# Attention and experts in one kernel: inputs laid out by superchunk and partition, and loads, masks and set-up moved

## The chip, the cores and the metric

The kernel runs on one core of one Trainium2 chip. The metric is the device time of one execution in microseconds (us); lower is better. A core has TensorE (PE, matrix products, with weight loads shown as PEld), VectorE (DVE), ScalarE (ACT), GpSimd (POOL) and SyncE (SP), which issues loads; 16 DMA engines move data between the main memory and SBUF. Products land in PSUM.

## What is computed

Sliding-window attention over 8 batches, 8 heads, 576 positions of 64 values, then a mixture of 8 experts over the 4,608 rows of 512 values. Cut to what matters:

```python
scores = scale * np.matmul(q, k.transpose(0, 1, 3, 2))
rel = pos[:, None] - pos[None, :]
mask = (rel >= 0) & (rel < 64)
attn = softmax(np.where(mask, scores, -1e9))
x = (attn @ v), as (batch, position, 512)

logits = x @ w_gate                       # 8 experts
local_gate = sigmoid(x @ w_local)
for s in range(S):
    fresh_e = argmax(logits[b, s])
    e = fresh_e if s == 0 or local_gate[b, s] < 0.5 else prev_e
    p = softmax(logits[b, s])
    out[b, s] = p[e] * (relu(x[b, s] @ w1[e]) @ w2[e])
```

A row's expert can be that of the row before it, so the routing runs along the sequence; all is in 32-bit floats.

## The kernel before

The rows are taken in 9 superchunks (`sc`) of 512 rows, each in 4 units (`hp`), a unit being two heads. A unit makes scores (36 small matmuls), an exponential on ScalarE, a multiplication by a 0/1 mask on VectorE, and then values (32 matmuls, with a column of ones that gives the row sum); VectorE divides and writes `x`. Scores run two units ahead (`LEAD = 2`). The values product takes v twice: `va` as loaded, and `vb`, the same rows displaced by 64, which ScalarE and GpSimd copy together from `va` of this superchunk and the one before (`shift`).

The gate logits come in one of two ways. For superchunks 0 to 3, x is transposed on TensorE (`turn`), multiplied by the gate weights (`gates`) and brought back (`logits`). From superchunk 4 (`TURNED`) on the gate product of v, loaded once more in transposed form (`vtt`), is put beside v as extra columns (`spread`), so that the values product delivers the logits as well. When the logits of the first 14 chunks of 128 rows are there, the routing of the first three batches (`Router.first`) runs in small steps beside the units that follow; the experts begin after attention.

Pools and loads (cut):

```python
    cp = ctx.enter_context(tc.tile_pool(name="at_const", bufs=1))
    kp = ctx.enter_context(tc.tile_pool(name="at_k", bufs=3))
    ps_s = ctx.enter_context(tc.tile_pool(name="at_ps_s", bufs=2, space=PSUM))
    ps_x = ctx.enter_context(tc.tile_pool(name="at_ps_x", bufs=2, space=PSUM))
    ctx.enter_context(tc.manual_schedule(engines={ET.PE, ET.Activation, ET.SP}))
    ...
    def space(name, sc):
        return kp.tile([P, 4, H, width(sc)], F32, name=name, bufs=2 if name == "vb" else 3)

    def load(sc, parts):
        t = slice(sc * SC, (sc + 1) * SC)
        src = v3[t] if sc < TURNED else v4[t.start - TURNED * SC:t.stop - TURNED * SC]
        for part in parts:
            if part == "turned":
                vtt = vts[sc] = kp.tile([P, HP, WIN + SC], F32, name="vtt", bufs=1)
                a = 0 if sc == TURNED else WIN
                at = (sc - TURNED) * SC + a
                nc.sync.dma_start(out=vtt[:, :, a:], in_=vt[:, :, at:at + WIN + SC - a])
            elif isinstance(part, tuple):
                ...
                nc.sync.dma_start(out=vas[sc][:, :, h], in_=src[:, h].rearrange("(c p) h x -> p c h x", p=P))
            else:
                if sc not in kts:
                    both = ring.tile([P, 2, HP, SC], F32, name="w")
                    kts[sc], qts[sc] = both[:, 0], both[:, 1]
                nc.sync.dma_start(out=kts[sc][:, part], in_=k[:, part, t])
                nc.sync.dma_start(out=qts[sc][:, part], in_=q[:, part, t])

    def until(i, x):          # a tiny load that holds SyncE until x is written
        nc.sync.dma_start(out=late[:, i:i + 1], in_=x)

    load(0, [slice(0, 1), slice(1, 2), (0, H // 2), pairs[1], (H // 2, H)])
    warm(20)                  # transposes of the identity, for TensorE's clock
    ...                       # both masks are built here, on VectorE
```

A row of k or q is 512 floats, 2,048 bytes; a row of v for 8 heads with its ones column is 2,080 bytes (2,368 with the gate columns). `ring` has four places of 2 MB, shared with the expert weights.

```python
    def shift(sc):
        va = vas[sc]
        vb = vbs[sc] = space("vb", sc)
        w = slice(width(sc - 1))
        nc.scalar.copy(vb[WIN:, 0, :, w], vas[sc - 1][WIN:, 3])       # L301
        nc.gpsimd.tensor_copy(vb[:WIN, :2], va[:WIN, :2])             # L302
        yield
        nc.scalar.copy(vb[WIN:, 1:3], va[WIN:, :2])                   # L304
        yield
        nc.gpsimd.tensor_copy(vb[:WIN, 2:], va[:WIN, 2:])             # L306
        yield
        nc.scalar.copy(vb[WIN:, 3], va[WIN:, 2])                      # L308

    # scores: matmuls L325, exponential L341, mask multiply L344
    # values: matmuls L354 into a tile of ps_x, reciprocal L359, x = L364
    # turn: transposes L249, copy L252; gates: L261/L263, copy gs L268; back: L273
    for u in units[:LEAD]:
        ps[u] = scores(*u)
        warm(16)
    shift_first(0)            # the first half of vb for superchunk 0: GpSimd L316, ScalarE L317
    until(0, masks[0][:1, :1])
    load(1, [pairs[0], whole, pairs[1]])

    for i, (sc, hp) in enumerate(units):
        if 1 < i < len(units) - LEAD:
            ps[units[i + LEAD]] = scores(*units[i + LEAD])
        if hp == 1 and sc + 1 < NSC:
            moves = shift(sc + 1)
        for _ in range(2):
            next(moves, None) if moves else None
        ...                   # at hp 3: spread, turn; at hp 0, 1, 2: turn, gates, logits of sc - 1
        step()                # a step of the routing, once it has begun
        values(sc, hp, ps.pop((sc, hp)), x, g)
        if i == 0:
            rt.prepare()      # the routing's constants, on GpSimd and VectorE
        ...
        if sc == 0 and hp == 2:
            until(1, allr[:1, 0, 2, 0, :1])      # the reciprocal of unit 2
            load(2, [pairs[0], whole, pairs[1]])
        if 0 < sc < NSC - 2 and hp in (0, 2):
            load(sc + 2, [pairs[1]] if hp else [whole, pairs[0]])
            if hp and sc + 2 >= TURNED:
                load(sc + 2, ["turned"])
```

The experts take their SBUF space when attention has given up its own; the first of them turns its rows on TensorE and copies them to `xt` (L1049), which the hidden product (L1190) reads:

```python
    def space(self, ctx):
        self.xq = ctx.enter_context(tc.tile_pool(name="ex_xq", bufs=6))
        self.wk = ctx.enter_context(tc.tile_pool(name="ex_work", bufs=2))
    ...
    def turn(self, st, quiet):
        st["xt"] = xt = self.wk.tile([P, DK, BIG], F32, name="xt")
```

Of the kernel before, what the change touches and what calls it, by code (L numbers as in the profile page):

```python
# [60 lines left out]
TURNED = 4  # L61
# [7 lines left out]
def kernel(  # L69
# [4 lines left out]
    v: bass.AP,  # L74
    v3: bass.AP,
    v4: bass.AP,
    vt: bass.AP,
    wg: bass.AP,
# [26 lines left out]
    with ExitStack() as fast:  # L105
        ring = fast.enter_context(tc.tile_pool(name="ring", bufs=4))
        rt = Router(fast, tc, lt, tabs, ident)
        ex = Experts(fast, tc, ring, *moe)
        zrow = ex.xp.tile([P, D], F32, name="xg")[:1]
        nc.vector.memset(zrow, 0.0)  # L110
        nc.gpsimd.dma_start(out=xs[N:N + 1, :], in_=zrow)
        attention(tc, ring, q, k, v3, v4, vt, xs, lt, ok, wgs, wg2s, ident, rt, ex)
        ex.run(fast, rt, lambda ps: flag(nc, ps, ok, bad, tabs["ej"][:, NBLK:], rare, ident))
# [34 lines left out]
def attention(ctx, tc, ring, q, k, v3, v4, vt, xs, lt, ok, wg, wg2, ident, rt, ex):  # L148
# [13 lines left out]
    nc = tc.nc  # L162
    cp = ctx.enter_context(tc.tile_pool(name="at_const", bufs=1))
# [4 lines left out]
    ps_x = ctx.enter_context(tc.tile_pool(name="at_ps_x", bufs=2, space=PSUM))  # L168
    ctx.enter_context(tc.manual_schedule(engines={ET.PE, ET.Activation, ET.SP}))

    qts, kts, vts, vas, vbs = {}, {}, {}, {}, {}

    def width(sc):
        return VX if sc < TURNED else VW

# [3 lines left out]
    def load(sc, parts):  # L179
        t = slice(sc * SC, (sc + 1) * SC)  # L180
        src = v3[t] if sc < TURNED else v4[t.start - TURNED * SC:t.stop - TURNED * SC]
        for part in parts:
            if part == "turned":
                vtt = vts[sc] = kp.tile([P, HP, WIN + SC], F32, name="vtt", bufs=1)

                a = 0 if sc == TURNED else WIN
                at = (sc - TURNED) * SC + a
                nc.sync.dma_start(out=vtt[:, :, a:], in_=vt[:, :, at:at + WIN + SC - a])
            elif isinstance(part, tuple):
                if sc not in vas:  # L190
                    vas[sc] = space("va", sc)
                h = slice(*part)
                nc.sync.dma_start(out=vas[sc][:, :, h], in_=src[:, h].rearrange("(c p) h x -> p c h x", p=P))
            else:
                if sc not in kts:
                    both = ring.tile([P, 2, HP, SC], F32, name="w")
                    kts[sc], qts[sc] = both[:, 0], both[:, 1]
                nc.sync.dma_start(out=kts[sc][:, part], in_=k[:, part, t])
                nc.sync.dma_start(out=qts[sc][:, part], in_=q[:, part, t])
# [11 lines left out]
    def warm(n):  # L211

        r = ps_x.tile([P, 2, SC], F32, name="xo")
        for _ in range(n):
            nc.tensor.transpose(r[:, 0, :P], ident, ident)

    warm(20)


# [11 lines left out]
    for i in range(2):  # L231
# [9 lines left out]

    allr = cp.tile([P, NSC, HP, 2, 4], F32, name="allr")

    def turn(sc, x, half):

        r = ps_x.tile([P, 2, SC], F32, name="xo")
# [8 lines left out]
    def gates(sc):  # L255

        r = ps_x.tile([P, 2, SC], F32, name="xo")
        for hp in range(HP):
            h = slice(hp * GW, (hp + 1) * GW)
            if sc < TURNED:  # L260
                nc.tensor.matmul(r[h, 0, :], lhsT=wg[:, hp, :], rhs=vts[sc][hp // 2][:, hp % 2], start=True, stop=True)  # L261
                continue
            nc.tensor.matmul(r[h, 0, :], lhsT=wg2[:, hp, :], rhs=vts[sc][:, hp, WIN:], start=True, stop=True)  # L263
            if sc == TURNED:
                nc.tensor.matmul(r[h, 1, :WIN], lhsT=wg2[:, hp, :], rhs=vts[sc][:, hp, :WIN], start=True, stop=True)
        n = SC + WIN if sc == TURNED else SC
# [14 lines left out]
    def spread(sc, gated):  # L281

        r, gs = gated
        by_head = back(r, gs).rearrange("p (c h g) -> p c h g", c=4, h=H)
        gt = by_head[:, :, :, :E + 1]
        g = slice(VX, VW)
        if sc == TURNED:
            o = r[:WIN, 0, :P]
            nc.tensor.transpose(o, gs[:, SC:], ident)
        nc.scalar.copy(vbs[sc][:WIN, :, :, g], gt[:WIN])  # L290
        nc.scalar.copy(vbs[sc][WIN:, 1:, :, g], gt[WIN:, :3])
        if sc == TURNED:
            nc.scalar.copy(vbs[sc][WIN:, 0, :, g], o.rearrange("p (h g) -> p h g", h=H)[:, :, :E + 1])
# [25 lines left out]
    def scores(sc, hp):  # L319
# [24 lines left out]
        nc.vector.tensor_tensor(p, p, m.to_broadcast([P, 2, SC]), op=Alu.mult)  # L344
        return p

    def values(sc, hp, p, x, g):
        va, vb, n = vas[sc], vbs[sc], width(sc)
        xo = ps_x.tile([P, 2, SC], F32, name="xo")
# [11 lines left out]
        if sc >= TURNED:  # L361
# [6 lines left out]
    ps = {}  # L368
    for u in units[:LEAD]:
        ps[u] = scores(*u)  # L370
        warm(16)
    shift_first(0)
    until(0, masks[0][:1, :1])
# [16 lines left out]
    def psum():  # L390
        return ps_x.tile([P, 2, SC], F32, name="xo")[:, 0, :]

    for i, (sc, hp) in enumerate(units):
        if hp == 0:
            x, g = wk.tile([P, 4, HP, 2, DH], F32, name="x"), None
            if sc >= TURNED:
# [4 lines left out]
        if hp == 1 and sc + 1 < NSC:  # L401
            moves = shift(sc + 1)
        for _ in range(2):
            next(moves, None) if moves else None
        if hp == HP - 1:
            if sc + 1 < NSC and sc + 1 >= TURNED:
                spread(sc + 1, gated)
            if sc < TURNED:
                turn(sc, x, 0)
                old = x  # L410
        elif 0 < sc <= TURNED:
# [7 lines left out]
        if side is None and 4 * sc >= C1 and hp >= (2 if sc == TURNED else 0):  # L419
# [3 lines left out]
        if i == 0:  # L423
            rt.prepare()
        if i < 2:
            ps[units[i + LEAD]] = scores(*units[i + LEAD])
            if i == 0:
                shift_first(1)
        if hp == 2 and TURNED <= sc + 1 < NSC:
            gated = gates(sc + 1)  # L430
        if sc == 0 and hp == 2:
            until(1, allr[:1, 0, 2, 0, :1])
            load(2, [pairs[0], whole, pairs[1]])
        if 0 < sc < NSC - 2 and hp in (0, 2):
            load(sc + 2, [pairs[1]] if hp else [whole, pairs[0]])
            if hp and sc + 2 >= TURNED:
                load(sc + 2, ["turned"])
# [7 lines left out]
        if hp == HP - 1:  # L445
            if sc >= TURNED:
# [550 lines left out]
class Experts:  # L997
# [44 lines left out]
    def turn(self, st, quiet):  # L1042
        nc, n = self.nc, st["rows"]
        st["xt"] = xt = self.wk.tile([P, DK, BIG], F32, name="xt")
# [184 lines left out]
    def space(self, ctx):  # L1229
        tc = self.tc  # L1230
        self.xq = ctx.enter_context(tc.tile_pool(name="ex_xq", bufs=6))
# [111 lines left out]
```

## Time and profile before

The median of three executions is 668.89 us (667.75 to 669.2); the profiled one has a span of 667.3 us.

| engine | busy, us | share of the span |
|---|---|---|
| TensorE, matmul | 633.9 | 95% |
| TensorE, weight load | 547.6 | 82% |
| VectorE | 384.5 | 58% |
| ScalarE | 177.7 | 27% |
| GpSimd | 123.8 | 19% |

Attention takes the first 146 us or so, the experts the rest. The DMA engines move 178.4 MB, on average 267 GB/s. Busy shares are means over both parts, so they are read by stretch. In a list of waits each line names who waited (engine and line of the kernel), for whom, and then the total in us, how often and the longest. In a timeline the first column is the start in us, the second the duration; brackets at the end give the idle time of the engine just before and what ended it. A wait called issue is one for which the profile shows no cause.

### The profile page before, as it was taken

The page shows a single profiled execution, that of the slowest core. Times are in us where ns is not written, and L with a number is a line of the kernel's source. Part 1 is how long each engine was busy: PE and PEld are TensorE (multiplying, and loading weights), DVE is VectorE, ACT ScalarE, POOL GpSimd, SP SyncE. Part 2 cuts the span into 40 slices and gives each one's busy share as a digit, 9 for nine tenths or more (in the row PEclk, how much of TensorE's full clock was granted, in tenths as well). Part 3 has the DMA queues.
Part 4 walks back from the last instruction along what each step waited for, and adds up shares of the span by engine and source line. Part 5 has one row for each costly group of instructions (what it writes and reads, how often), then busy time and mean ns, then how long its engine had stood idle before and what let it go on. Part 6 is the DMA issues. An engine that isn't in the chain of part 4 may idle for free. (4 is left out here: it accounts for less than half of the span.)

```text
span 667.3 us, 15133 instructions
## 1 busy us (share of the span) xinstructions
PE 633.9 (95%) x6537; PEld 547.6 (82%) x6537; DVE 384.5 (58%) x693; ACT 177.7 (27%) x274; POOL 123.8 (19%) x128
## 2 busy tenths in 40 slices
PE   8868887889999999999999999999999999999995
PEld 7757766677777789989989998999799979997983
DVE  6645589782961078448638753873566366636410
ACT  2646655431111222303221230312132213211200
POOL 4121112311124111113112211401221121101011
PEclk9989999899999999999999999999999999999998
DMA  8699999999887976577559557764865586457540
GB/s 302 215 383 382 320 371 370 374 353 383 317 301 278 370 281 218 224 281 288 209 174 400 192 217 284 289 237 170 308 227 206 181 316 246 169 182 287 210 153 24
DMA packets 34415, 178.38 MB, mean 267 GB/s; under 512 B 3325, under 2 KB 4355, under 8 KB 27428
## 3 DMA queue, kind: packets, MB, share of 16 engines
q1 hardware_dynamic: 25524, 147.82, 60.6%
q0 software_dynamic: 8816, 29.50, 11.2%
q8 instruction: 54, 0.88, 0.5%
q14 instruction: 21, 0.17, 0.1%
HBM read 158.43 MB, written 19.40 MB: 267 GB/s over the span
## 5 line engine op out<-in xcount | busy, mean ns | idle before, releaser
L1172 POOL DMA_INDIRECT out_dram<-y,idx x36 | 39.9, 1107 | 300.7 <-DVE y L1151 140.8
L1190 PEld LDWEIGHTS hp<-xt,w 128*128 128x128 f32 (+1 forms) x1152 | 88.2, 168 | 4.6 <-issue 3.1
L1190 PE MATMUL hp<-xt,w 128*128 128x128 f32 (+1 forms) x1152 | 89.4, 252 | 1.2 <-ACT xt L1049 1.2
L1099 PE MATMUL hp<-xs,ws 128*128 128x128 f32 x624 | 73.9, 275 | 0.0
L1099 PEld LDWEIGHTS hp<-xs,ws 128*128 128x128 f32 x624 | 71.8, 192 | 0.0
L1142 PE MATMUL hp<-ws,hs 128*128 128x256 f32 x312 | 71.6, 379 | 0.0
L1221 PE MATMUL yp<-w,h 128*128 128x512 f32 x160 | 70.9, 594 | 0.0
L1023 POOL DMA_INDIRECT xg<-xs,idx x40 | 47.2, 1179 | 115.5 <-PE tp L1048 78.8
L1142 PEld LDWEIGHTS hp<-ws,hs 128*128 128x128 f32 x312 | 59.3, 190 | 8.1
L344 DVE TENSOR_TENSOR p<-p,mask 128x1024 f32<-128x1024 f32 x36 | 46.0, 1283 | 23.8 <-ACT p L341 23.6
L1221 PEld LDWEIGHTS yp<-w,h 128*128 128x128 f32 x160 | 29.5, 190 | 32.6 <-issue 31.8
L1110 DVE TENSOR_TENSOR h<-hp,keep 128x512 f32<-128x512 f32 x39 | 27.0, 691 | 49.2 <-PE hp L1099 49.2
L354 PEld LDWEIGHTS xo<-vb,p 128*64 128x64 f32 x576 | 39.0, 139 | 17.4 <-issue 6.1
L354 PE MATMUL xo<-vb,p 128*64 128x74 f32 (+1 forms) x576 | 44.6, 230 | 8.2 <-DVE va L294 2.0
L1099 PEld LDWEIGHTS hp<-xt,w 128*128 128x128 f32 x416 | 49.3, 192 | 3.4 <-issue 2.3
L1099 PE MATMUL hp<-xt,w 128*128 128x128 f32 x416 | 51.0, 276 | 0.0
L341 ACT ACTIVATE p<-sp 128x1024 f32<-128x1024 f32 x36 | 36.8, 1025 | 51.4 <-PE sp L325 46.7
L1151 DVE SCALAR_TENSOR_TENSOR y<-hp,pw,kept 128x256 f32<-128x256 f32 x39 | 18.3, 481 | 55.9 <-issue 33.7
L1142 PE MATMUL hp<-w,h 128*128 128x256 f32 x208 | 49.5, 381 | 0.0
L325 PE MATMUL sp<-w 64*64 64x128 f32 (+1 forms) x1296 | 42.9, 270 | 4.6 <-issue 2.9
L325 PEld LDWEIGHTS sp<-w 64*64 64x64 f32 x1296 | 37.4, 138 | 11.8 <-issue 7.0
L354 PE MATMUL xo<-va,p 128*64 128x74 f32 (+1 forms) x576 | 44.8, 230 | 0.8 <-issue 0.8
(268 smaller groups left out, 905.1 us busy)
## 6 DMA issues: line engine op xcount, KB each, us to landing
w<-in_w_dram SPq DMA_DIRECT2D x54, 2048.0 KB, 8.8
xs<-x POOLq DMA_DIRECT2D x9, 1024.0 KB, 11.5
w<-in_k_dram SPq DMA_DIRECT2D x17, 512.0 KB, 11.3
w<-in_q_dram SPq DMA_DIRECT2D x17, 512.0 KB, 12.1
va<-in_v_dram SPq DMA_DIRECT2D x5, 1184.0 KB, 6.7
vtt<-in_vt_dram SPq DMA_DIRECT2D x4, 1024.0 KB, 7.2
va<-in_v_dram SPq DMA_DIRECT2D x3, 1040.0 KB, 11.8
vtt<-in_vt_dram SPq DMA_DIRECT2D x1, 1152.0 KB
```

The costliest lines, as they stand in the source:

```text
L325: nc.tensor.matmul(sp[c * WIN:(c + 1) * WIN, j, a:b], lhsT=kt[h, hp, block * WIN:(block + 1) * WIN], rhs=qt[h, hp, a:b], start=True, stop= ...
L341: nc.scalar.activation(p, sp, Act.Exp, scale=DH ** -0.5)
L344: nc.vector.tensor_tensor(p, p, m.to_broadcast([P, 2, SC]), op=Alu.mult)
L354: nc.tensor.matmul(xo[par * WIN:(par + 1) * WIN, j, s * VW:s * VW + n], lhsT=p[:, j, b * WIN:(b + 1) * WIN], rhs=w[:, s, 2 * hp + j, :n], ...
L1023: self.nc.gpsimd.indirect_dma_start(out=x, out_offset=None, in_=self.xs[:rows, :], in_offset=bass.IndirectOffsetOnAxis(ap=idx[:, s:s + 1], ...
L1099: nc.tensor.matmul(out[:, m, :], lhsT=a[:, kk, m * P:(m + 1) * P], rhs=b[:, kk, :], start=start and m + kk == 0, stop=stop and (m, kk) == ...
L1110: nc.vector.tensor_tensor(o, x, y, op=add)
L1142: nc.tensor.matmul(out, lhsT=a[:, m, :], rhs=b[:, m, :], start=start and m == 0, stop=stop and m == FK // 2 - 1, skip_group_check=True)
L1151: nc.vector.scalar_tensor_tensor(y[i][:, j * w:(j + 1) * w], x, pw[i], y2, Alu.mult, Alu.add)
L1172: self.nc.gpsimd.indirect_dma_start(out=self.out[:, :], out_offset=bass.IndirectOffsetOnAxis(ap=st["idx"][:, s:s + 1], axis=0), in_=y, in_ ...
L1190: nc.tensor.matmul(hp[a, i, :], lhsT=st["w1"][:, kk, m * P:(m + 1) * P][:, a], rhs=st["xt"][:, kk, :n], start=(kk == 0), stop=(kk == DK - 1))
L1221: nc.tensor.matmul(yp, lhsT=st["h"][:, m, :P], rhs=st["w2"][:, m, :], start=(m == 0), stop=(m == FK - 1))
```

## The change

k and q of a superchunk come from one array in which, for each superchunk and partition, the rows for a pair of units lie together: a load of two units' k and q has rows of 8,192 bytes and is one transfer in place of two (4,096 bytes for the two single units at the start). v is stored by superchunk and partition as well: rows of 8,320 bytes, or 9,472 with gate columns; loads of half the heads keep pieces of 1,040 bytes. The transposed v gets rows of 8,192 bytes, and its 64 leading columns a small array and load of their own. The bytes are the same.

Besides this, the third superchunk's loads wait for unit 0 in place of unit 2; the second mask is built after the second unit's mask multiply, and the routing's constants at unit 8 in place of unit 0; the warm-up transposes are 12 and 24 in place of 20 and twice 16; the shift of v begins one unit earlier (for superchunk 1, all of it in unit 3); the ScalarE copy for the leading columns comes first among those of `spread`; the two PSUM tiles of `ps_x` become two pools used strictly in turns; and `xt` of the experts has a pool of its own, allocated first, as the pool of the transposed v is in attention. It is for feeding attention earlier and keeping TensorE from waiting. The diff, cut:

```diff
-TURNED = 4
+GATED = range(4, NSC)
+    tp = ctx.enter_context(tc.tile_pool(name="at_t", bufs=1))
     cp = ctx.enter_context(tc.tile_pool(name="at_const", bufs=1))
...
-    ps_x = ctx.enter_context(tc.tile_pool(name="at_ps_x", bufs=2, space=PSUM))
+    ps_x = [ctx.enter_context(tc.tile_pool(name=f"at_ps_x{i}", bufs=1, space=PSUM)) for i in range(2)]
+
+    def bank():
+        ps_x.reverse()
+        return ps_x[0].tile([P, 2, SC], F32, name="xo")
...
-                vtt = vts[sc] = kp.tile([P, HP, WIN + SC], F32, name="vtt", bufs=1)
-                a = 0 if sc == TURNED else WIN
-                at = (sc - TURNED) * SC + a
-                nc.sync.dma_start(out=vtt[:, :, a:], in_=vt[:, :, at:at + WIN + SC - a])
+                t = tp.tile([P, HP * (SC + WIN)], F32, name="vtt")
+                vts[sc] = main, ahead = t[:, :HP * SC], t[:, HP * SC:]
+                nc.sync.dma_start(out=main, in_=vt[GATED.index(sc)].rearrange("p h x -> p (h x)"))
+                if sc - 1 not in GATED:
+                    nc.sync.dma_start(out=ahead, in_=vh.rearrange("p h x -> p (h x)"))
...
-                nc.sync.dma_start(out=vas[sc][:, :, h], in_=src[:, h].rearrange("(c p) h x -> p c h x", p=P))
+                src, h = v4[GATED.index(sc)] if sc in GATED else v3[sc], slice(*part)
+                nc.sync.dma_start(out=vas[sc][:, :, h], in_=src[:, :, h])
...
-                    both = ring.tile([P, 2, HP, SC], F32, name="w")
-                    kts[sc], qts[sc] = both[:, 0], both[:, 1]
-                nc.sync.dma_start(out=kts[sc][:, part], in_=k[:, part, t])
-                nc.sync.dma_start(out=qts[sc][:, part], in_=q[:, part, t])
+                    kqs[sc] = ring.tile([P, HP, 2, SC], F32, name="w")
+                    kts[sc], qts[sc] = kqs[sc][:, :, 0], kqs[sc][:, :, 1]
+                nc.sync.dma_start(out=kqs[sc][:, part], in_=kq[sc, :, part])
...
-    warm(20)
+    warm(12)
...
+    build_mask(0)
...
     for u in units[:LEAD]:
         ps[u] = scores(*u)
-        warm(16)
     shift_first(0)
+    with tc.issue_after(masked[-1].ins):
+        build_mask(1)
+    warm(24)
     until(0, masks[0][:1, :1])
...
-        if hp == 1 and sc + 1 < NSC:
+        if hp == (0 if sc else 3) and sc + 1 < NSC:
             moves = shift(sc + 1)
-        for _ in range(2):
+        for _ in range(2 if sc else 4):
             next(moves, None) if moves else None
...
-        if i == 0:
-            rt.prepare()
...
-            if i == 0:
-                shift_first(1)
+        if i == 0:
+            shift_first(1)
+            until(1, allr[:1, 0, 0, 0, :1])
+            load(2, [pairs[0], whole, pairs[1]])
+        if i == 2 * HP:
+            with tc.issue_after(masked[-1].ins):
+                rt.prepare()
...
-        if sc == 0 and hp == 2:
-            until(1, allr[:1, 0, 2, 0, :1])
-            load(2, [pairs[0], whole, pairs[1]])
...
-        st["xt"] = xt = self.wk.tile([P, DK, BIG], F32, name="xt")
+        st["xt"] = xt = self.xtp.tile([P, DK, BIG], F32, name="xt")
...
+        self.xtp = ctx.enter_context(tc.tile_pool(name="ex_xt", bufs=2))
         self.xq = ctx.enter_context(tc.tile_pool(name="ex_xq", bufs=6))
```

`issue_after` orders the block's VectorE instructions behind the named one. The arrays on the host are reordered to match.

## The prediction

> **What bounds the kernel now.** I first read the page's slices, then busy time by stretch, then TensorE's waits, then the waits of the engines it waits for.
>
> ```profile
> PE   8868887889999999999999999999999999999995
> PEclk9989999899999999999999999999999999999998
> DMA  8699999999887976577559557764865586457540
> ```
>
> A slice is 16.7 us. From slice 9 on (146 us) TensorE never falls below 9 tenths. The same by stretch (busy us of TensorE matmul and weight load, VectorE, ScalarE, GpSimd, then granted clock, DMA share, GB/s):
>
> ```profile
> 0.00:14.00 14.00, 10.93 (x124) 10.05 (x124) 8.95 (x34) 4.17 (x4) 6.33 (x23) 1.00 0.84 285
> 14.00:48.00 34.00, 26.62 (x650) 23.25 (x652) 19.03 (x27) 18.41 (x21) 8.23 (x9) 0.95 0.84 301
> 48.00:146.00 98.00, 82.11 (x1944) 66.64 (x1940) 75.54 (x190) 53.02 (x69) 20.44 (x20) 0.98 0.99 360
> 146.00:667.00 521.00, 514.20 (x3828) 447.67 (x3828) 281.00 (x445) 102.07 (x181) 88.84 (x78) 1.00 0.66 247
> ```
>
> The experts (146 us to the end) lose 521.0 - 514.2 = 6.8 us, and the stretch 660 to 667.3 has only 0.20 us of matmul, so that is the tail. Nothing in the diff shortens this part: whatever attention wins arrives undiminished at the end, whatever it doesn't touch stays. In attention TensorE idles 14.0 - 10.9 = 3.1, 34.0 - 26.6 = 7.4 and 98.0 - 82.1 = 15.9 us; and much of the first 10.9 is warm-up transposes. TensorE's waits up to 146 us:
>
> ```profile
> PE xo L273 <- ACT gs L268: 6.0, 4, 5.0
> PE sp L325 <- issue: 2.9, 3, 1.4
> PE xo L215 <- POOL ident masks.py:199: 2.6, 1, 2.6
> PE xo L354 <- DVE va L294: 2.0, 1, 2.0
> ...
> PE sp L325 <- ACT p L341: 1.6, 1, 1.6
> PE xo L354 <- ACT p L252: 1.5, 1, 1.5
> PE hp L1190 <- ACT xt L1049: 1.2, 1, 1.2
> ```
>
> The largest single one is 5.0 us. ScalarE's own timeline says why (start, duration, line, idle before it):
>
> ```profile
> 31.82 0.62 ACT L301 COPY vb<-va 64x520 f32<-64x520 f32 x1
> 37.12 1.05 ACT L304 COPY vb<-va 64x1040 f32<-64x1040 f32 x1 [4.68 <-DMA va<-in_v_dram]
> 38.20 0.59 ACT L268 COPY gs<-xo 128x512 f32<-128x512 f32 x1
> ```
>
> The copy of the gate product stands in ScalarE's queue behind a shift copy, which waits for the third superchunk's v. That load was issued at 26.1 us only, because SyncE was held by unit 2:
>
> ```profile
> SPq L205 <- DVE allr L359: 12.2, 1, 12.2
> ```
>
> Meanwhile the DMA was empty: 20 to 26 us show a DMA share of 0.10 and 34 GB/s. And the wait costs twice: from 39.8 to 43.2 us the granted clock is 0.63. The values and score groups there take 2.01 and 1.32 us where their neighbours take 1.15 and 1.12.
>
> **What the Trainium skill says.** TensorE: Matmul & The Clock Gate, section "What's actually happening": the array falls to half clock after an idle window of about 3.4 us. This trace agrees: 5.03 us idle, then 0.63. Perfetto Trace Analysis, "DMA Optimizations": small transfers, to about 2 KB, carry overhead, and going to 4 or 8 KB helps, "dramatically". The trace shows less: 14 to 20 us (k, q and v in rows of some 2 KB) move 382 GB/s at a share of 1.03, or 371 per full share; 220 to 230 us (weights in rows of 16 KB) 410 at 1.02, or 402. So 8% is the most. The same page, "Matmuls": independent groups should rotate through PSUM banks, so that evacuation lies beside the next group. The trace has waits of that kind, of 1.5 us (L354 on L252) and 2.0 us (on L294).
>
> **The change, part by part.**
>
> 1. *Start.* The first value product runs at 14.04 us. Its last wait is the mask multiply L344, which starts at 12.67, though its exponentials were ready at 9.81 (8.78 + 1.03): VectorE was in the routing set-up from 10.69 to 12.79, which itself waited for GpSimd. Moving that set-up and the second mask (1.79 us) behind the multiplies leaves the chain: scores of unit 0 (now after 12 warm-up transposes in place of 20; at 4.53/20 = 0.23 us each they end near 5.3), scores of unit 1 when its k and q land (they run at 10.50 now; issued at 1.73 and 2.20 us, with a median of 4.4 to 5.6 us to landing for such loads, they are there near 7 to 8, and the 16 transposes between are gone), exponentials to 9.7, shift copy L317 0.84 to 10.6, warm-up to about 11.6. So 14.0 becomes about 11.6: 2.4 us.
>
> 2. *Third superchunk.* The gate moves from unit 2's reciprocal (24.25 us) to unit 0's. That one now has the second mask ahead of it on VectorE, so it ends near 13. Loads go out from about 14 and queue behind the second superchunk's, without the hole of 6 us. Bytes up to the third v: first and second superchunk 2 x 3.16 MB, k and q of two pairs 1.05, v 1.06, together 8.4 MB, 8.6 with small ones. 2.5 MB are through at 10 us (249 GB/s in 0 to 10), the rest goes at about 0.41 MB/us, an estimate from the 402 to 410 of the weights: 24.9 us. Landing lags by 1.9 us now (the GB/s in steps of 2 us add up to 5.5 MB, the bytes to the second v, at 17.9 us, and the copy that needs it starts at 19.84). So the third v lands near 26.8 in place of 37.1.
>
> 3. *What TensorE does with it.* The second superchunk's shift is now at unit 3, so its copies (0.62 + 1.05 + 0.62) no longer hold the exponentials back at 20.3 us (the 1.6 us wait on L341 goes). In exchange they delay the turn copy there, about 1 us. With 1.15 us for values, 1.12 for scores and 1.09 for a turn, unit (1,0) comes near 25. The third superchunk's shift starts at the same unit and waits for 26.8: over 1 us, then its copy (1.05) and the turn copy (1.01), gates from 28.9, then gates 1.07, values 1.15, scores 1.12, the way back 0.66 and values of unit (1,2) to 34.0. Now they end at 41.88: 7.9 us, with the clock loss in it, plus 0.2 from the next score group. **Sum of 1 to 3: 8.1 us.** The 2.4 us of the start are in it, not beside it, for the third v is the last to come.
>
> 4. *From there to 142 us.* Shift one unit earlier for all later superchunks: takes ScalarE work from the unit of the gate copies (waits of 0.25 to 0.34 us), puts it into that of the turn copies; even. PSUM in turns and the small halo copy put first: of the 1.5 us on L252, some 0.4 (the two copies of the other bank end at 74.9, not 75.2). Routing set-up at unit 8: at most 2.1 us of small VectorE work, with the multiplies two units ahead: nothing. Longer rows: DMA is full here (0.99) but no engine waits for a load in this stretch, so nothing but slack. I take **0.5 us**.
>
> 5. *First expert.* Its copy xt waits 3.72 us for the last value products, by my reading because its SBUF space was attention's. A space of its own, lying over the turned v that is done long before, ends the wait: **1.2 us** (the last line above).
>
> Sum 8.1 + 0.5 + 1.2 = 9.8, so 668.9 - 9.8 = 659.1; rounded, **659.0 us**.
>
> **The rivals.** *A: the DMA takes over as the bound.* For it: share 0.99 over 98 us; a superchunk from the fifth on moves 2.1 + 1.2 + 1.05 + 1.05 = 5.4 MB, at 0.37 to 0.38 MB/us some 14.5 us, and TensorE's pace now is 13.4 to 16.5 us. Against: there are no waits on loads in it, and rows of 8 KB take the loads' part down by up to 8% (about 13.6 us). If it came, the 8.1 us would shrink to some 4 to 5: 664. *B: the opening stays as it is*, for the second v's landing at 19.8 us sets it and rows of 1,040 bytes in the first half loads stay. Then only the hole counts, 5.0 + 1.3 + 1.2 and little else: 661. *C: more than I count.* The four waits that the profile calls issue in 60 to 137 us (5.2 us; together with a clock of 0.87 in 110 to 120) would go if they came from a full DMA: 653. They have no releaser in the profile, and long packets might as well lengthen them: that is the way up, too.
>
> **Range and chances.** Mine 659, A 664, B 661, C 653; the times before lie within 1.5 us. 8 in 10: 653 to 665. Faster by over 2% needs 655.5, C or an opening better than mine: 0.18. Slower by over 2% needs a new stall of 23 us: 0.02.
>
> **What would show it.** Right: values of unit 0 at 11 to 12 us; no DMA slice below 8 tenths before 60 us; the wait of L273 on gs under 1.5 us; no clock of 0.6 at 40 us; the L1190 wait gone; attention over at about 136 us, the experts as long as before. Wrong: new waits on DMA w or va in 20 to 60 us (A), the wait of the turn copy over 2 us (step 3), more than 6.8 us idle after attention, or gaps of issue that grow.

## The result and the profile after

The changed kernel takes **663.85 us** (median of 4 runs, 661.59 to 664.44) where the kernel before takes 668.6 on the same chip: a ratio of 0.992, 95% interval 0.990 to 0.995. In a second set of runs it took 662.9 against 667.3, a ratio of 0.994 (0.992 to 0.996). So 4.4 to 4.8 us are gained. The prediction said 659.0, a gain of 9.8: its range holds the result, and half of its gain isn't there.

The slices of the profile after, in the order of those before:

```profile
PE   7888878999999999999999999999999999999996
PEclk9999998999999999999999999999999999999998
DMA  9989989999878967487468657755865586457540
```

The 8 tenths of clock that stood third are gone, and the second DMA slice has 9 tenths in place of 6 (the third 8 in place of 9). By stretch, with the borders moved to where the same work now lies (columns as before):

```profile
0.00:14.00 14.00, 11.41 (x218) 10.64 (x222) 9.23 (x20) 5.21 (x6) 6.36 (x22) 1.00 0.88 325
14.00:40.00 26.00, 21.72 (x528) 18.27 (x522) 17.13 (x24) 16.61 (x19) 8.21 (x8) 1.00 0.91 367
40.00:140.00 100.00, 83.51 (x1967) 68.25 (x1967) 77.20 (x206) 53.85 (x70) 21.18 (x22) 0.98 0.93 351
140.00:661.90 521.90, 514.17 (x3824) 448.21 (x3823) 281.86 (x446) 102.07 (x181) 86.54 (x78) 1.00 0.66 248
```

From 14 to 40 us TensorE idles 26.0 - 21.7 = 4.3 us, where it idled 7.4 up to 48. From 40 to 140 it idles 16.5, a little more than the 15.9 of before. TensorE's waits up to 146 us:

```profile
PE xo L364 <- DVE va L304: 5.3, 3, 2.1
...
PE xo L273 <- ACT p L262: 2.4, 4, 0.8
PE sp L335 <- issue: 2.0, 3, 1.0
PE xo L364 <- issue: 1.9, 2, 1.0
PE xo L364 <- DVE lt L291: 1.9, 4, 0.5
...
PE sp L335 <- ACT p L351: 1.2, 1, 1.2
...
PE r L739 <- DVE vk L732: 1.1, 1, 1.1
```

The 5.0 us behind the gate copy are gone, and so is the 1.5 on the turn copy. New on top: values products that wait for the gates' spread copies (L304, 2.0 before, 5.3 now), gate products behind the turn copy (L262, none before), values products behind the logits reduction (L291, none before), and in the experts the second routing's transposes (L739). ScalarE round the third superchunk's shift:

```profile
24.58 0.62 ACT L311 COPY vb<-va 64x520 f32<-64x520 f32 x1
25.90 1.05 ACT L314 COPY vb<-va 64x1040 f32<-64x1040 f32 x1 [0.70 <-DMA va<-in_v_dram]
26.98 1.01 ACT L262 COPY p<-xo 128x1024 f32<-128x1024 f32 x1
27.89 1.03 ACT L351 ACTIVATE p<-sp 128x1024 f32<-128x1024 f32 x1
28.94 0.62 ACT L318 COPY vb<-va 64x520 f32<-64x520 f32 x1
29.59 0.59 ACT L280 COPY gs<-xo 128x512 f32<-128x512 f32 x1
```

The shift copy that waited 4.68 us for the third v and ran at 37.1 now waits 0.70 and runs at 25.9. SyncE opens the gate after 5.4 us of waiting in place of 12.2.

**Where the gain is made and lost.** The reciprocal that follows each unit's values product is a mark for TensorE's progress (start in us; "again" is a second execution of the changed kernel):

```
unit                     before    after   gain    again   gain
(0,0)                     15.80    13.14    2.7    14.19    1.6
(1,2)                     41.92    34.75    7.2    34.85    7.1
(3,3)                     76.50    70.28    6.2    69.56    6.9
(4,3)                     92.71    88.09    4.6    86.37    6.3
(8,3), the last          144.77   139.40    5.4   137.36    7.4
first hidden product     145.94   139.28    6.7   137.25    8.7
from there to the end    521.35   522.65   -1.3   522.67   -1.3
end                      667.28   661.93    5.4   659.92    7.4
```

The opening brings 7.2 us. Between (1,2) and the last unit the first execution gives 1.8 of them back, the second nothing; the wait at the first expert goes (+1.3), and the experts themselves take 1.3 longer in both.

### The profile page after: what moved, and what is told of

It reads as the page before. It is cut to its first block, busy times and chain, and to the rows that moved or that the text cites. A ratio compares the mean times of both kernels' runs of the same rounds, so it can differ in the third digit from the quotient of the medians.

```text
span 661.9 us, 15065 instructions
## 1 busy us (share of the span) xinstructions
PE 630.8 (95%) x6521; PEld 545.4 (82%) x6521; DVE 385.4 (58%) x693; ACT 177.7 (27%) x274; POOL 122.3 (18%) x128
## 5 line engine op out<-in xcount | busy, mean ns | idle before, releaser
L1185 POOL DMA_INDIRECT out_dram<-y,idx x36 | 38.2, 1061 | 301.1 <-DVE y L1164 141.9
L354 DVE TENSOR_TENSOR p<-p,mask 128x1024 f32<-128x1024 f32 x36 | 47.4, 1320 | 20.5 <-ACT p L351 20.2
## 6 DMA issues: line engine op xcount, KB each, us to landing
w<-in_kq_dram SPq DMA_DIRECT2D x17, 1024.0 KB, 10.5
va<-in_v_dram SPq DMA_DIRECT2D x3, 1040.0 KB, 11.5
va<-in_v_dram SPq DMA_DIRECT2D x2, 520.0 KB, 10.3
```

What stands on the lines that cost most here:

```text
L354: masked.append(nc.vector.tensor_tensor(p, p, m.to_broadcast([P, 2, SC]), op=Alu.mult))
L1185: self.nc.gpsimd.indirect_dma_start(out=self.out[:, :], out_offset=bass.IndirectOffsetOnAxis(ap=st["idx"][:, s:s + 1], axis=0), in_=y, in_ ...
```

## The experiments

**Theory T**: the opening's gain is the earlier gate's, helped by the earlier first unit; half of the rest of the prediction was lost because the strict turns of PSUM and the shift one unit earlier made waits of their own, and because the wait at the first expert moved to the second routing. **Rivals**: D, the loads set the end of attention, whatever the waits are called; V, VectorE or ScalarE sets the pace between 60 and 120 us; L, the long rows made the gain; F, formed on the way: TensorE runs short of instructions where nothing else holds it up. First the middle.

**One pool in place of turns.**

```diff
-    ps_x = [ctx.enter_context(tc.tile_pool(name=f"at_ps_x{i}", bufs=1, space=PSUM)) for i in range(2)]
+    ps_x = ctx.enter_context(tc.tile_pool(name="at_ps_x", bufs=2, space=PSUM))
     def bank():
-        ps_x.reverse()
-        return ps_x[0].tile([P, 2, SC], F32, name="xo")
+        return ps_x.tile([P, 2, SC], F32, name="xo")
```

> The changed kernel with the two PSUM tiles again in one pool of two, in the order that the build chooses. Theory T (the PSUM tiles in strict turns and the earlier shift each brought new waits, some 3 to 5 us in all, which ate half of the gain of the opening): the four waits of the values product on the logits reduction (0.47 us each) and the one of 2.1 us on the gate copy at unit (4,3) go, but the build's choice may bring others in the first two superchunks; 661 to 663 us against 663.9. Rival D (DMA is the bound after 40 us, so waits on PSUM only stand where a wait on data would stand): 663.5 to 664.5. Rival V (VectorE sets the pace from 80 to 120 us, where its busy share is 0.95 and more): no change, 663.5 to 664.5.

Measured: 662.2 us, ratio 0.992 (0.990 to 0.994). The waits on L291 are gone and the spread copies are back at 2.0 us, but a wait of 1.6 behind the turn copy is back too, and the first hidden product waits 1.4 for the last x. The turns do make the waits that T names; taking them out is worth nothing that this shows.

**Turns, but skipped** after each logits product and at (4,3), so that the next values product takes the tile that is free already.

```diff
         gt = back(*gated).rearrange("p (c h g) -> p c g h", c=4, h=HP)[:, :, :E + 1]
+        ps_x.reverse()
...
+        if (sc, hp) == (4, HP - 1):
+            ps_x.reverse()
         values(sc, hp, ps.pop((sc, hp)), x, g)
```

> The changed kernel with turns, except that the values product after each way back of the logits, and that of unit (4,3), takes the tile that was free, as the kernel before did. Theory T: the four waits of 0.47 us and most of the 2.1 us go, nothing else moves; 660 to 661.5 us. Rivals D and V: 663.5 to 664.5.

Measured: 662.95 us, 0.992 (0.989 to 0.995). The waits on L291 went from 1.9 to 0 and those on the spread copies from 5.3 to 3.2, as T says. But the waits called issue grew to 8.6 us from 14 to 139 us, from 4.5. That is what called for F (one of them, 2.3 us, turns out below to be a wait for VectorE).

**The shift back at the second head pair** for superchunks 2 to 8.

```diff
-        if hp == (0 if sc else 3) and sc + 1 < NSC:
+        if hp == (1 if sc else 3) and sc + 1 < NSC:
             moves = shift(sc + 1)
```

> The changed kernel with the shift of superchunks 2 to 8 again from the second unit. Theory T: the four waits of the gate products on the turn copy (2.4 us in all) go and those on the gate copy (some 0.3 us each, three or four times) come back; 662 to 663 us. Rival D: a later shift costs nothing and gains nothing, 663.5 to 664.5. Rival V: the same.

Measured: 662.1 us, 0.991 (0.989 to 0.993). The gate products no longer wait for the turn copy (2.2 us before the edit); 0.6 us behind the gate copy came instead. The mechanism is right; the gain, 0.9 us by the ratio of the changed kernel above and 1.9 by that of its second set, is inside the uncertainty.

**Both repairs**, beside the changed kernel itself, which ran again without an edit:

> The changed kernel once more, without an edit, on the same chip as the three that follow, so that their times stand beside one of its own. Every theory: 663 to 665 us, about 0.993 of before. Its profile is a second execution of the same stream: the waits that belong to the new order (the spread copies of L304 5.3 us in 38.6 to 138 us, the logits reduction of L291 1.9, the gates' products behind the turn copies 2.2, the second routing's transposes behind DVE vk 1.05) should be there again within 0.3 us each, and the waits called issue may differ by 2 us or more.

Measured: 662.9 us, 0.994 (0.992 to 0.996), its profile is of the fastest of six runs, 1.3 us under their median. L304 5.3, L262 2.2, L291 1.4, vk 1.1 us: the waits are the stream's own.

```diff
+    ps_x.reverse()                                          # ahead of everything
...                                                          # and both edits above:
         gt = back(*gated).rearrange("p (c h g) -> p c g h", c=4, h=HP)[:, :, :E + 1]
+        ps_x.reverse()
-        if hp == (0 if sc else 3) and sc + 1 < NSC:
+        if hp == (1 if sc else 3) and sc + 1 < NSC:
...
+        if (sc, hp) == (4, HP - 1):
+            ps_x.reverse()
```

> Both repairs of attention in one: the turns skipped after each logits product and at (4,3), and the shift of superchunks 2 to 8 back at the second head pair. Theory T (the new waits in the middle are made by the turns and the earlier shift): waits on L291 0, on the spread copies about 3 us in place of 5.3, turn copies before the gates' products 0 in place of 2.2; the last reciprocal starts about 4 us earlier than in the changed kernel (135 to 136 us in place of 139.4) and the time is 3 to 5 us shorter: 659 to 661 us. Theory V (VectorE or ScalarE sets the pace in 60 to 120 us, and waits only change their names): the other waits grow by as much, the last reciprocal stays within 1 us of 139.4 and the time within 1.5 us of the changed kernel's. Theory D (loads set the end of attention after 40 us): no change either, and waits on DMA va and w appear.

Measured: ratio 0.993 (0.991 to 0.996), level with the changed kernel; seven of the times lie in two groups, three at 659.2 to 661.3 and four at 663.5 to 664.6 (an eighth was disturbed). TensorE's waits from 38.6 to 138 us in it:

```profile
PE xo L366 <- issue: 3.2, 2, 2.2
PE xo L276 <- issue: 2.3, 1, 2.3
PE xo L366 <- DVE va L306: 1.6, 2, 1.2
PE sp L337 <- issue: 1.5, 1, 1.5
PE xo L366 <- DVE t L893: 1.2, 1, 1.2
```

The named waits are down as T expected (1.6 on the spread copies, none on the reduction or the turn copies), and the issue lines have taken their place: 7.0 us. The last reciprocal starts at 137.3, level with the 137.4 of the changed kernel's second execution. So T's expectation for the time fell here. D doesn't explain it: no wait on a load shows. V explains one line. The gap of 2.3 us stands before a gate product (L276), whose semaphore wait in the trace ends at 110.94, just after VectorE's semaphore of 110.90; VectorE had just read the values product before it out of PSUM (L376, after a routing product of 1.49 us and a mask multiply of 1.22):

```profile
110.21 0.68 DVE L376 TENSOR_TENSOR x<-xo,allr 128x512 f32<-128x512 f32 x1
110.99 1.08 PE L276 MATMUL xo<-vtt,wg2s 128*32 128x512 f32 x4 [2.25 <-issue]
```

So "issue" says only that the list names no releaser; this gap has one. The other 4.7 us are of another kind.

**One pool and the shift back.**

```diff
-    ps_x = [ctx.enter_context(tc.tile_pool(name=f"at_ps_x{i}", bufs=1, space=PSUM)) for i in range(2)]
+    ps_x = ctx.enter_context(tc.tile_pool(name="at_ps_x", bufs=2, space=PSUM))
...
-        if hp == (0 if sc else 3) and sc + 1 < NSC:
+        if hp == (1 if sc else 3) and sc + 1 < NSC:
```

> The changed kernel with both repairs of the middle in another form: one pool of two PSUM tiles in place of the strict turns, and the shift of superchunks 2 to 8 at the second head pair. Theory T (turns and earlier shift each made waits of their own): no waits on the logits reduction, none of the gates' products behind the turn copies, the last reciprocal at 135 to 137 us, 659.5 to 661 us, 2 to 4 us under the changed kernel. Theory F (without those waits TensorE uses up its instructions faster, and the gaps without any wait, which in all profiles so far stand at every 256th of its instructions, grow in their place): these gaps sum to 6 us or more in 14 to 139 us in place of 4 to 5, and the time is within 1.5 us of the changed kernel's.

Measured: 661.15 us (4 runs, 660.9 to 663.5), 0.989 (0.987 to 0.991), 2 to 3 us under the changed kernel by the ratios, and clear of the interval of its second set of runs, though not of the first; the two were not timed side by side. The profile is of the slowest of the four; TensorE's waits from 14 to 139 us, first lines:

```profile
PE xo L363 <- issue: 5.4, 3, 3.2
PE sp L334 <- issue: 2.2, 4, 0.9
PE xo L363 <- DVE va L303: 2.0, 1, 2.0
```

In time T was right this time. In the profile F was: 8.6 us of issue, 8.4 of it of the kind described next, more than in any other profile, with one gap of 3.2 us.

**What issue is.** The page lists a DMA queue that nothing in the kernel's text fills (packets, MB, share of 16 engines), here in the kernel after:

```profile
q8 instruction: 53, 0.87, 0.5%
```

0.87 MB in 53 packets is 16 KB each, and TensorE has 2 x 6521 = 13,042 matmuls and weight loads on the page: one packet for some 250. In the trace's own list of TensorE's instructions (matmuls, weight loads and the few semaphore instructions between them, counted in order of start from 0), 67 of the 75 issue gaps of over 0.3 us between 14 and 139 us, in all 14 profiles, stand ahead of a number 193 or 194 + 256 n. Of the other eight, three of 0.35 to 0.37 us stand at the last gate product, and five of 1.1 to 2.3 us at the one before it; these five end some 0.09 us after VectorE's semaphore, like the one above, and are counted here as waits with a releaser:

```
kernel                TensorE's waits       gaps at 256-marks    longest
(14 to 139 us)        with a releaser, us   number, sum us       us
third gate late          19.0                  3, 2.0             0.8
before                   17.3                  5, 4.6             1.4
short rows               17.1                  6, 3.2             1.1
xt shared                16.6                  1, 1.0             1.0
after                    15.9                  5, 3.9             1.0
after, again             13.6                  6, 5.2             1.3
shift back               13.4                  2, 1.5             1.2
old opening              13.1                  4, 4.7             2.2
gate alone               12.3                  5, 4.6             1.7
one pool                 11.9                  4, 3.1             1.7
turns skipped            11.5                  6, 6.0             1.6
both, routing later      11.3                  7, 6.2             1.7
one pool + shift         10.1                  7, 8.4             3.2
skipped + shift           8.0                  6, 7.2             2.2
```

Each of the 67 ends 2.16 to 2.59 us after the start of a packet of this queue. So TensorE's instructions come in blocks of 256, and a gap is TensorE at the end of a block whose successor isn't there yet. The Trainium skill has the block: Runtime: NRT & Kernel Launch, "Instruction fetch mechanics", says that instructions are refilled in blocks of 16 KiB, 256 of them, by a DMA queue of their own while the current block runs, and that the cost of crossing into the next is "mostly hidden". The traces agree on block and queue, not on hidden: 1.0 to 8.4 us of 125 here, where TensorE uses up most blocks in 4 to 8 us. A packet mostly starts 1 to 5 us after TensorE has entered the block before it; what sets that start isn't seen. The table's two middle columns run against each other, loosely (correlation -0.7): that a real wait gives the next block time to arrive, and a wait removed is paid back in part, fits this but isn't shown, for no run changed the fetching alone.

**Waits and gaps apart.** Between two reciprocals the gaps at the marks can be taken off, an estimate that counts each in full:

```
                    (1,2) to (5,0)   gaps at marks   without them   (5,0) to (6,2)
before                 53.7              1.4            52.4            23.2
after                  56.9              2.5            54.3            23.2
after, again           55.0              1.1            54.0            23.2
xt shared              53.4              0.0            53.4            23.2
shift back             55.3              1.2            54.1            23.2
one pool               54.0              1.0            53.0            24.0
turns skipped          55.4              2.2            53.2            23.8
one pool + shift       54.3              2.8            51.5            23.2
skipped + shift        53.3              2.5            50.8            25.5
```

The kernel with xt shared (next experiment) has the changed kernel's attention, so three lines show one stream: with the same named waits it takes 53.4 to 56.9 us, and most of the spread is gaps. Without the gaps the stream lies 1.1 to 2.0 us over before, and the two pairs of repairs 2 to 3.5 us under it. So T's mechanism is there; part of its gain went into gaps, 2.5 to 2.8 us in the two pairs where the stream has 0 to 2.5. From (5,0) to (6,2), where the routing runs beside attention, V holds: in 11 of the 14 profiles, before among them, the stretch takes 23.2 to 23.3 us, of which VectorE is busy for 22.5, whatever TensorE waits for. A gap of 1.5 us at a mark there in the kernel with the old opening made it no longer; one of 2.2 us just at its beginning (90.6 to 92.8 us) in skipped + shift did, with VectorE only 0.47 busy from 90 to 95 us.

**The experts.** First the space of xt, back in the pool that it shared.

```diff
-        st["xt"] = xt = self.xtp.tile([P, DK, BIG], F32, name="xt")
+        st["xt"] = xt = self.wk.tile([P, DK, BIG], F32, name="xt")
```

> The changed kernel with the first expert's xt again in the experts' working pool. By the prediction's step 5 it is slower by 1.2 us: 665.1. Theory R (the 1.2 us were won at the first hidden product and lost again 5 us later, where the second routing's transposes now wait 1.05 us for VectorE): the wait of 1.2 us comes back, that of 1.05 us goes, 663.5 to 664.3.

Measured: 667.4 us, 0.999 (0.997 to 1.000), 3 to 4 us slower than the changed kernel. The waits from 138 to 150 us (the first columns are who waited for whom):

```profile
ACT xt L1062 <- DVE f L472: 6.3, 1, 6.3
DVE ts L741 <- PE r L739: 4.1, 1, 4.1
...
PE hp L1203 <- ACT xt L1062: 3.3, 1, 3.3
```

With a shared pool, xt lies where attention's very last check (f) is, waits 6.3 us, and TensorE 3.3. The clock follows (TensorE alone: busy, clock, DMA share, GB/s):

```profile
139.50:145.00 5.50, 5.50 (x36) 0.69 1.00 396
145.00:150.00 5.00, 5.00 (x41) 1.00 0.85 314
```

and the first 32 hidden products take 5.47 us in place of 3.84; on the other side, the wait of 1.1 for vk is gone. From the last reciprocal to the end this kernel takes 526.0 us, the one with the next edit 521.4 and the other twelve profiles 522.0 to 523.0. So in the new layout the space is worth three times the 1.2 us, but as a loss avoided; set against the kernel before it brings nothing, as the table of marks says.

Then the second routing's transposes one step of hidden products later, on top of both repairs.

```diff
+        pause += STEP        # in the experts' loop, after the first step of the routing
```

> The run with both repairs, and in the experts the second routing's transposes asked one step of hidden products later. Theory T with the experts' part (the 1.05 us behind DVE vk is idle time that nothing later makes up): no wait of those transposes, the rest after the first hidden product about 521.4 us in place of 522.5, and the time 1 us under that of the run with both repairs alone. Rival R (the routing's later end comes back as a wait of the second half's products or of a gather, or the wait is only shifted): the rest stays within 0.4 us of the one without this edit.

Measured: **660.7 us**, 0.990 (0.987 to 0.992); the rest after the first hidden product is 521.54 us in place of 522.35, and the wait for vk is gone. That is the 0.8 to 1 us expected; the median lies 2.8 under its twin's 663.5 (of those seven), and what goes beyond 1 us is within the spread of the two. With the pool variant above it is the best version of this study, 6.6 us under the kernel before.

**The opening.** The gate alone, put back to unit (0,2):

```diff
-            until(1, allr[:1, 0, 0, 0, :1])       # after the first unit
-            load(2, [pairs[0], whole, pairs[1]])
+        if sc == 0 and hp == 2:
+            until(1, allr[:1, 0, 2, 0, :1])
+            load(2, [pairs[0], whole, pairs[1]])
```

> The changed kernel with the third superchunk's loads gated by the unit (0,2) again, all else as changed. Theory T (the earlier gate is what the opening's gain rests on: the third v lands near 26 us in place of 37): the POOL and ACT copies of L314 wait for DMA va until 32 to 34 us, the values of (1,2) end 5 to 7 us later, and the time is 4 to 6 us longer: 668 to 670 us, all of the gain gone. Rival A (the longer rows and the earlier start of unit 0 carry the gain and the transfers have slack anyway): at most 2 us longer, 664 to 666 us.

Measured: 666.2 us, 0.999 (0.997 to 1.000), 3.3 us slower than the changed kernel beside it. ScalarE waits 5.6 us for the third v again (the line is its, from 14 to 50 us) and the clock falls to 0.66 between 30 and 40 us:

```profile
ACT vb L314 <- DMA va<-in_v_dram: 5.6, 1, 5.6
```
```profile
30.00:40.00 10.00, 6.70 (x94) 4.61 (x96) 2.72 (x5) 5.22 (x6) 2.04 (x2) 0.66 1.02 422
```

The reciprocal of (1,2) comes at 40.85, 6.0 later than in the changed kernel's run beside it, the last one 3 to 5 us later: from 41 us on this kernel has 2 issue gaps fewer and catches up. In the medians 3.3 us are left: less than T's 4 to 6, more than A's 2. The mechanism is T's, and the gate carries more of the opening's gain than the other two parts below.

**The gate alone, in the kernel before.**

```diff
+                until(1, allr[:1, 0, 0, 0, :1])       # beside shift_first(1), at i == 0
+                load(2, [pairs[0], whole, pairs[1]])
-        if sc == 0 and hp == 2:
-            until(1, allr[:1, 0, 2, 0, :1])
-            load(2, [pairs[0], whole, pairs[1]])
```

> The kernel before with one edit: the third superchunk's loads are gated by the unit (0,0) in place of (0,2). Theory T (the gate is most of the opening's gain, and needs neither the longer rows nor the rest): the values of (1,2) end 3 to 5 us earlier than before's 41.9 and, as the new waits of the middle are not in this kernel, nearly all of it stays: 663 to 665 us, level with the changed kernel. Rival L (in rows of 2 KB the transfers have no room before 30 us, and the earlier v and w push back those of the second superchunk): a new wait on DMA w or va at (1,0) or (1,1), and the time within 1.5 us of before's 667 to 668.

Measured: 665.7 us, 0.996 (0.994 to 0.998): one moved gate is worth 2.7 us (1.7 to 3.8), by the medians more than half of the whole change, though less than T's 3 to 5; (1,2) comes 2.5 us earlier. The rows of 2 KB have room for it. The stretch 20 to 30 us went from a DMA share of 0.43 to this:

```profile
20.00:30.00 10.00, 6.85 (x146) 5.89 (x147) 6.83 (x8) 7.17 (x8) 3.29 (x4) 1.00 1.05 386
```

**Short rows, everything else as changed** (excerpt; v and the turned v likewise in the rows of the kernel before).

```diff
-                nc.sync.dma_start(out=kqs[sc][:, part], in_=kq[sc, :, part])
+                for n in range(2):
+                    nc.sync.dma_start(out=kqs[sc][:, part, n], in_=kq[sc, :, part, n])
```

> The changed kernel with its inputs in the old rows of about 2 KB (k and q in separate transfers, v and vt by head pair), the earlier gate, masks, turns and shift all kept. Theory T (the earlier gate makes the opening's gain, the longer rows only add some per cent of rate): the first values product within 0.5 us of the changed kernel's, the third v lands 1 to 3 us later, the reciprocal of (2,0) 1 to 2 us later, the time 1 to 2 us longer than the changed kernel's 663 to 664. Rival L (the long rows carry the gain; with 34 thousand packets the transfers that now start earlier collide): the waits for DMA va at the third superchunk come back with 4 us or more and the time is 5 us longer, 668 to 669. Rival S (rows have no effect at all): within 1 us.

Measured: 665.9 us, 0.997 (0.995 to 0.999), 2 to 3 us slower than the changed kernel by the ratios. The same stretch in the two (this kernel first, then the changed one):

```profile
20.00:30.00 10.00, 7.36 (x156) 6.10 (x160) 5.65 (x7) 8.00 (x10) 4.21 (x5) 1.00 1.05 389
```
```profile
20.00:30.00 10.00, 8.58 (x191) 6.76 (x189) 6.38 (x8) 9.15 (x12) 4.24 (x5) 1.00 1.02 426
```

389 against 426 GB/s at a full DMA. The third v's copy runs at 27.4 in place of 25.9, the reciprocal of (2,0) 1.8 us later. T's size, or a little over it; L and S fall. The short rows come with twice as many transfers of k and q, and the run doesn't part the two.

**The old opening, everything else as changed.**

```diff
-    warm(12)
+    warm(20)
...
+    build_mask(1)
...
-    with tc.issue_after(masked[-1].ins):
-        build_mask(1)
-    warm(24)
...
+        if i == 0:
+            rt.prepare()
```

> The changed kernel with the opening of before: warm-up of 20, 16 and 16, both masks built ahead of the first unit, the routing's set-up at the first unit. Theory T (the second mask and the set-up stood ahead of the first spread copies on VectorE and GpSimd): the first values product 2 to 3 us later (12.5 to 13.5 in place of 10.5), and as the third superchunk's gate opens with that unit the whole attention 2 to 3 us later: 666 us. Rival B (the delay is absorbed, as the loads in 20 to 40 us set the pace): the reciprocal of (2,0) within 1 us of the changed kernel's 41.2 and the time within 1 us.

Measured: 665.2 us, 0.997 (0.995 to 0.998), 2 to 3 us slower than the changed kernel by the ratios. The first values product runs at 13.2 in place of 10.5 to 11.5, the reciprocal of (1,2) at 37.7 in place of 34.8, the last at 142.6. T's direction and size. The profile is of an execution 1.9 us over the median, so its last mark is a late one.

The three parts of the opening, undone one by one at (1,2), cost 6.0 (gate), 2.8 (masks, set-up, warm-up) and 1.5 us (rows), together 10.3 where all bring 7.2. They overlap; that a load which comes earlier helps only as far as the first unit and the bandwidth allow is my reading of it.

## Why the prediction was half right

- **The reading of before**, the third v behind the gate with an empty DMA ahead of it: right. The late gate brings back the 5.6 us wait and the low clock; the gate alone brings 2.7 us to the old kernel.
- **Steps 1 to 3, 8.1 us: 7.2.** First values product 11.6 expected, 10.5 and 11.5 measured. Third v 26.8 expected, 25.9 measured. Values of (1,2) over at 34.0 expected, 34.7 measured, and 1.0 us of that is the fetch gap within this very group (33.21 to 34.21), which no step counted.
- **Step 4, +0.5 us: this step failed, at -1.8 us** in the profile of after (+0.3 in the second and +1.8 in xt shared, each the quickest execution of its set; by the medians some 2.5 us are missing, if the opening brought 7.2 there too). "Even", it said of the earlier shift, and took only the gain of the turns. New waits it didn't see: 3.3 us on the spread copies, 2.2 on the turn copy ahead of the gate products, 1.4 on the logits reduction (38.6 to 138 us), against 1.5 and 0.9 saved; the turn copy's was on the prediction's own list of wrong signs, with 2 us, and came to 2.4. The cause of the first and third is shown by the runs that undid the turns (5.3 to 2.0 or 3.2, 1.9 to 0): a strict alternation gives a values product the tile that the product just before filled, though the other has been free for a while. The old pool gave the free one. From (1,2) to (5,0) these waits cost some 1.1 to 2.0 us net; the rest is gaps at block ends (2.5, 1.1 and 0 us in the three executions, 1.4 before), which no step had.
- **Step 5, +1.2 us: net 0.** The wait at the first expert is gone, as said. But VectorE needs 143.91 + 0.12 - 139.79 = 4.2 us from the last x to vk, TensorE has 32 hidden products of 3.84 us to run ahead of the transposes that read vk, and having started 1.3 us sooner it waits 1.1 there. The prediction took "whatever attention wins arrives undiminished" without asking what else hangs on VectorE's last product. Delaying those transposes gets 0.8 us of it back.
- **The sum** of one profile: 7.2 - 1.8 + 1.3 - 1.3 = 5.4, and 667.28 - 661.93 = 5.35 us.
- **Rival A** (transfers take over): no. After 40 us the DMA share is 0.93, lower than before, and no wait of TensorE on a load exceeds 1.0 us in any profile. Rival B (only the hole counts): its 661 is nearer than 659, but its reason fell, as the first unit did come earlier and it mattered. **Rival C** named the issue waits (five, not four, make up its 5.2 us) and supposed a full DMA behind them; four stand at block ends, one is a wait for VectorE, and such gaps stayed.
- **Left open:** what sets the start of a block's fetch, and so why one stream has 0 to 2.5 us of gaps in the same stretch; and why one pair of repairs shows 2 to 3 us in the times and the other none.

## What to carry to other kernels

A load gate that leaves the DMA idle for 6 us is worth moving before anything else: moving it alone gave, by the medians, more than half of what this whole change gave. Before you add up waits to be removed, look whether another engine is busy all through the stretch (VectorE for 22.5 of 23.2 us here): there it made no difference what TensorE waited for. And count the engine's instructions: where it used up a block of 256 in 4 to 8 us, gaps without a releaser came to 1.0 to 8.4 us and differed between executions of one stream, so give the sum of removed waits a range. And where two tiles alternate, ask which was read last, not which was written last; strict turns can hand out the one that is still being read.

## What the runs showed of the hardware

- TensorE's gaps without a releaser stand at every 256th instruction (67 of 75), 0.3 to 3.2 us each; one stream had 0, 1.1 and 2.5 us of them in one stretch of three executions.
- A wait of 3.3 us left the clock at 0.69 in the 5.5 us after it: 32 products took 5.47 us in place of 3.84. So the 3.3 cost 4.9, before what it hid (the wait of 1.1 for vk).
- Rows four times as long (8 KB for 2 KB), in fewer transfers, went with 426 in place of 389 GB/s at a full DMA, 9% (20 to 30 us, one profile each); the prediction had taken 8% as the most.
